# A new list of steps, other first transfers, and a 128-row product in place of a 6-row one, in a fused attention and feed-forward kernel

## The chip, the cores and the metric

One core of a Trainium2 chip runs the whole kernel. The metric is the device time of one execution in microseconds. Several runs are timed and their median is given; one further execution is profiled, and its trace is what is read here. The core has a matrix engine (TensorE, PE in the views; its weight loads, PEld, run beside the products), VectorE (DVE), ScalarE (ACT), GpSimd (POOL) and SyncE (SP, which issues the transfers).

## The reference

```python
# q, k, v: (8, 8, 576, 64) f32
scores = q @ k.T / sqrt(64)                       # per batch and head
rel = pos[:, None] - pos[None, :]
mask = (rel >= 0) & (rel < 32)                    # heads 0 to 3
mask = (rel >= 0) & (rel < 128) & (rel % 4 == 0)  # heads 4 to 7
attn = softmax(where(mask, scores, -1e9))
x = (attn @ v).transpose(0, 2, 1, 3).reshape(4608, 512)
h = x @ w_in                                      # (512, 2048), f64 given
g = h * tanh(softplus(h))                         # Mish
out = g @ w_out                                   # (2048, 512), f64 given
```

## The kernel before

The 4608 tokens are cut into 16 units of 288 (half a batch each). A unit is loaded, its scores, softmax and values are computed in four pairs of heads, the result is transposed to become the feed-forward's input, and two layers follow. In the feed-forward every number is carried as a high and a low f16 part, so that a product becomes three f16 products; the attention does the same from unit 3 on, and in f32 for units 0 to 2. From unit 4 on, two units at a time go through the first layer in a form with seven products for eight.

All engines' work is given in one list, the string `ORDER`. Each word is a step, and its instructions are issued in the list's order on each engine's own queue; a word that stands several times continues the step to its next `yield`. A number behind `=` says which of several buffers or PSUM banks (`banks`, four) the step takes. The engines wait for each other by semaphores, so a list changes when things can run, not what runs. The steps that matter here:

- `kw4`, `kw8`, `kw12`: so many products of zeros on TensorE (`keep_warm`, L1167), which nobody reads.
- `ld0`, `ld1`: q and k of a unit (L480 to L491); `lv`: its v (L511, L513). `wl0.0.1`: one block of weights, 2 x 512 KB, into one of four raw buffers (`w_load`, L372).
- `wm`, `wa` (ScalarE, L389 and L396), `ww` (VectorE, L442, L444), `ws` (TensorE L410, column sums, then VectorE), `wp` (ScalarE L455, VectorE L458): they turn a block of f64 weights into two f16 parts. `ws` needs both blocks of its group, and a raw buffer is free when `wp` is done.
- `sp`, `sc` (TensorE L680 and L683: mask and scores; VectorE L713: their maxima), `tp` (for units 0 and 1 the scores again, transposed, less the maxima, L816, then Exp), `va` (values), `tx` (transpose of the result).
- `pr`: a unit's scales. `largest` (L349) transposes the partitions' maxima (L352), reduces them (L355), puts them on the diagonal of a tile `dg` (L357) and multiplies that by ones (L360), so that every partition has them. It has 2 columns for units 0 and 1 and 6 for units 3 to 15; unit 2 goes another way.
- `ff` (first layer, L1111, units 0 to 3), `fo` (second layer, L1138), `gt` (L1126 and L1128), `ex` (Exp, units 2 and up), `za` to `zg` (first layer from unit 4 on, L1023; they and `ff` use Mish).

`wl` waits on SyncE for its raw buffer, and whatever stands behind it in SyncE's queue waits too.

Of the kernel before, what the change touches and what calls it, by code (L numbers as in the profile page):

```python
# [47 lines left out]
ld1 tp0.3=2 wp0.0.0 va0.0 kw4=1 wa0.3.1 kw8=1 ws0.3=1 tp0.3=0 va0.0=0 va0.1=2 va0.3=2 tx0.0=0 ws0.3 xa0.1=2 va0.3
wp0.3.0 va0.2=1 kw4=3 wl0.2.0=0 kw4=3 va0.2 tx0.0 sp1.1=3 tx0.0 va0.3=0 wp0.3.1 wp0.3.0 va0.2=1 sp1.0=2 sc1.1 tx0.1=1
sp1.2=3 sc1.0 tp1.0=2 tx0.0 wp0.3.1 wl0.2.1=1 wm0.2.0=0 sc1.2 tx0.1 ww0.2.0 ww0.2.0 wm0.2.1=0 tx0.1 tx0.1 ww0.2.1  # L50
wl0.1.1=2 wa0.2.0 ww0.2.1 tp1.0=1 wa0.2.1 wm0.1.1=0 wl0.1.0=3 tp1.2=0 lv2 sp1.3=3 wm0.1.0=0 sc1.3 ff0.6=1 xa1.0=3
ws0.2=2 ws0.2 ww0.1.0 ff0.7=3 ff0.7 pr1=0 ww0.1.1 ws0.1=2 ff0.6 tp1.2=0 ws0.1 pr1=0 pr1 ff0.0=2 wp0.2.0 wp0.2.1 pr1=0
wp0.2.0 ff0.0 pr1 fs0 ff0.6=0 ff0.7 va1.2=0 ff0.0=1 va1.0=1 wl1.2.0=0 va1.0 va1.2 wp0.2.1 tp1.3=3 tp1.3=1 ff0.1=2
ww0.1.1 wp0.1.1 va1.0=1 wl1.2.1=1 va1.2=3 ww0.1.0 wm1.2.0 wp0.1.1 tp1.1=3 ww1.2.0 tp1.1=0 wp0.1.0 wp0.1.0 ld2 va1.3=1
ff0.1 va1.3 va1.1=0 fs1 wm1.2.1 ff0.4=3 va1.3=2 ff0.4 va1.1 wl1.3.1=2 ff0.1 gt0.3=4 ww1.2.1 ff0.4=2 va1.1=0 ws1.2=1
tx1.0=0 ww1.2.1 tx1.0 ws1.2 tx1.1=2 ff0.5=3 ww1.2.0 gt0.3 ff0.5 tx1.1 tx1.1 gt0.0=3 tx1.0 wl1.3.0=3 pr2 ff0.2=1 ff0.5
tx1.1 ff0.2 ff0.3=3 xa3.0=4 ff0.3 wp1.2.0 wp1.2.0 tx1.0 wp1.2.1 wp1.2.1 sp2.3=2 wm1.3.0 ww1.3.0 gt0.0 sp2.1=0 ff0.2=0
ff0.3 wl1.0.0=0 sc2.3=0 sc2.1=1 wm1.3.1 gt0.2=0 ff1.2=1 ff1.6=3 ff1.6 ex2.3 ff1.2 ww1.3.1 ws1.3=2 wl1.1.1=1 ww1.3.0
ex2.1 ff1.7=0 ff1.7 gt0.2 ff1.2=1 ff1.6=2 ws1.3 gt0.1=2 wp1.3.0 tp2.3=2 ww1.3.1 sp2.2=1 ff1.7 wp1.3.0 ff1.3=3 gt0.1
sc2.2=3 ff1.3 tp2.3=1 wf1.1=0 xa2.1=1 pr2=0 pr2 wm1.0.0 ww1.0.0 wf1.1 fo0.2.0=2 wm1.1.1 ww1.1.1 fo0.2.1 sp2.0=0 ff1.3  # L60
ex2.2 fo0.2.2 sc2.0=2 wl1.0.1=3 wm1.0.1 wp1.3.1 ww1.0.1 tp2.1=3 tp2.1=0 fo0.3.0 va2.3=1 ex2.0 wp1.3.1 ww1.0.1 fo0.3.1
tp2.2=3 gt1.1=1 gt1.1 tp2.2=1 va2.1=0 ws1.0=3 va2.1 va2.3 va2.1=1 fo0.3.2 gt1.3=5 fo0.3.3 fo0.3.3=1 ws1.0 wp1.0.1
wf1.1=1 ww1.0.0 va2.2=0 va2.2 fo0.2.3 ld3 ff1.0=3 ff1.0 gt1.3 wl1.1.0=2 wm1.1.0 va2.3=0 ff1.1=1 va2.2=3 ff1.0=2 fs2
ww1.1.0 wp1.0.0 ws1.1=0 tx2.1=3 ff1.1 fo0.2.3=0 ww1.1.1 ww1.1.0 tx2.1 xa2.0=2 ws1.1 ff1.1 gt1.0=6 ff1.5=2 tx2.1 wf1.1
tx2.1 ff1.4=1 ff1.4 wp1.0.0 fo0.0.0=0 tp2.0=3 wp1.1.1 wp1.1.0 tp2.0=1 wp1.1.1 wp1.1.0 wf1.1 ff1.5 va2.0=3 ff1.4=0
ff1.5 gt1.2=7 gt1.0 lv3 wp1.0.1 fo0.0.1 fo0.0.2 wf0.0=2 gt1.2 va2.0 fo0.0.3 va2.0=3 tx2.0=2 ol pr3 pr3 fo0.2.3
fo1.2.0=1 fo1.2.1 wf1.0=0 pr3 pr3=3 wf0.0 fo0.0.3=0 mr fo0.3.3 wf1.0 fo0.0.3 fo1.2.2 pr3 pr3=3 wf0.0=1 wf0.0 pr3
fo1.2.3 pr3 fo0.1.0 xw3.0=1 wf0.1=2 pr3 pr3 wf0.0 fo1.2.3=1 fo1.2.3 pr3 pr3 ld4 fo0.1.1 fo0.1.2 fo0.1.3 pr3 tx2.0
sp3.1=3 fo1.3.0 fo1.3.1 wf1.0=1 pr3 lv4 fo0.1.3=0 sp3.0=0 tx2.0 sc3.1=2 ex3.1 tp3.1=0 pr4 sp3.3=2 sc3.3=0 fo1.3.2
fo1.3.3 sp3.2=2 fo1.0.0=3 fo1.0.1 pr4 fo1.1.0 tp3.1 ex3.3 sc3.0=1 tp3.3=1 pr4 fs3 fo1.3.3=1 ex3.0 ff2.0=0 ff2.0 wf1.0  # L70
sc3.2=3 pr4=2 pr4 tp3.1=0 xa3.1=3 ff2.1=1 wf1.0 ff2.1 tp3.0=0 tp3.0 va3.1=2 fo1.0.2 ex3.2 ff2.0=0 ff2.1 pr4=0 va3.1
wf0.1 tp3.3 pr4 va3.1 fo0.1.3 tp3.0=1 gt2.0=4 pr4 gt2.0 pr4 pr4 fo1.0.3 ff2.4=1 ff2.4 tp3.3=0 ff2.4=1 pr4 pr4 va3.0=0
tp3.2=1 fo1.3.3 pr4 ff2.5=2 ff2.5 fo1.0.3=0 ff2.5 ld5 fo1.1.1 tp3.2 tp3.2=1 sp4.0=1 fo1.1.2 va3.0 fo1.1.3 wf0.1=0
ff2.6=2 pr4 lv5 sc4.0=1 wf0.1 wf0.1 ff2.2=1 fo1.1.3=1 wf2.1=2 va3.0 xw3.1=0 va3.2=3 gt2.2=3 ex4.0 pr5 pr5 tp4.0=0
va3.2 zx3.0=0 va3.3=0 va3.3 wf2.1 va3.2 ff2.6 ff2.2 pr5 gt2.2 wf2.1=1 ff2.3=3 va3.3 zx3.0 zx3.1=1 pr5=0 wf2.1 ff2.2=2
pr5 ff2.3 ff2.3 gt2.1=2 tp4.0 fo2.2.0=0 zx3.0 pr5=3 sp4.3=1 zx3.1 zx3.1 pr5 pr5 fo2.3.0 xw4.0=2 ff2.6=0 ff2.7=3
sp4.1=2 pr5 sc4.3=2 ff2.7 sc4.1=0 gt2.1 ex4.3 fo2.0.0=1 ff2.7 ff3.2=2 ff3.2 pr5 pr5 pr5 tp4.0=1 fo2.1.0 wf2.1 ff3.2=2
ld6 pr5 sp4.2=3 sc4.2=3 sp5.0=2 xw5.0=3 fo1.1.3 fs4 fo2.2.1 va4.0=3 sc5.0=1 fo2.3.1 fo2.2.2 ff3.3=2 ex4.1 ex4.2
fo1.0.3 ex5.0 pr5 lv6 tp4.1=1 tp4.1 tp4.1=0 tp5.0=0 wf2.0=1 gt2.3=0 gt2.3 pr6 va4.0 ff3.3 ff3.3 tp5.0 fo2.1.1 fo2.1.2
fo2.1.3 va4.0 tp5.0=1 fo2.1.3=0 sp5.1=3 fo2.1.3 pr6 wf2.0 sp5.3=2 wf2.0=0 sc5.3=0 ex5.3 wf2.0 fo2.0.1 wf2.0 fo2.0.2  # L80
fo2.0.3 va4.1=2 va4.1 fo2.2.3 fo2.0.3=1 fo2.0.3 tp4.2=1 sp5.2=1 sc5.1=1 gt3.1=1 ff3.4=3 ex5.1 va4.1 gt3.1 tp5.1=0
tp5.1 ff3.4 ff3.4=1 tp5.1=0 fo2.2.3=0 ff3.5=2 va5.0=3 fo2.2.3 va5.0 tp4.2 sc5.2=1 ex5.2 ff3.5 tp4.2=1 zl2.1=0 wf3.0=2
# [1146 lines left out]
```

## Time and profile before

| | before |
|---|---|
| device time, median of 3 runs | 871.92 us |
| its runs | 871.92, 870.03, 872.19 us |
| the profiled execution's own time | 870.22 us |
| its span in the profile | 868.4 us |
| TensorE busy | 858.3 us (99%) |
| ScalarE, VectorE busy | 676.0 us (78%), 665.4 us (77%) |
| mean granted TensorE clock | 0.998 |

The span is from the first to the last instruction. TensorE's busy time is modelled from pipelined products, so that 99% does not tell how dense they are; idle time before an instruction and what ended it do. The granted clock is a share of 2.4 GHz; 0.50 is 1.2 GHz.

### The profile page before, as it was taken

How to read it: one execution, taken by the hardware profiler on the slowest of the kernel's cores; microseconds unless marked ns; L12 is line 12 of the kernel's file. 1: busy time of each engine (PE TensorE's matmuls, PEld its weight loads, DVE VectorE, ACT ScalarE, POOL GpSimd, SP SyncE). 2: the span in 40 equal slices, each digit the busy share in tenths (PEclk: the TensorE clock that was granted, in tenths of full speed). 3: DMA queues.
4: the chain of work that ended last, by engine and by line, in shares of the span. 5: the costliest groups of instructions: out<-in, count | busy, mean ns of one | idle time of the engine just before them, and what ended most of it. 6: DMA issues, size and time to landing. Idle time of an engine off the chain costs nothing.

```text
span 868.4 us, 21528 instructions
## 1 busy us (share of the span) xinstructions
PE 858.3 (99%) x8976; PEld 691.0 (80%) x8979; DVE 665.4 (77%) x1034; ACT 676.0 (78%) x978; POOL 18.5 (2%) x93
## 2 busy tenths in 40 slices
...
GB/s 257 291 192 213 131 69 158 132 176 151 142 181 192 216 196 155 216 129 174 232 144 193 167 176 173 198 166 200 189 125 181 120 188 123 132 110 155 105 8 48
DMA packets 211009, 141.20 MB, mean 163 GB/s; under 512 B 151392, under 2 KB 195936, under 8 KB 210912
## 3 DMA queue, kind: packets, MB, share of 16 engines
...
## 4 chain that ended last, share of the span: by engine, by line
PE 70%; DVE 5%; ACT 1%; issue 1%; DMA 0%; SPq 0%; DVEq 0%; ACTq 0%
PE b L1138 35%; PE b L1023 29%; PE b L857 3%; PE b L683 3%; DVE g L1128 1%; DVE p L787 1%; DVE sb L707 0%; DVE nm L713 0%; DMA out_T<-y 0%; DVE hm L969 0%; PE b L1111 0%; DVE sb L715 0%; ACT L1114 0%; ACT hm L1114 0%; DVE g L1008 0%
## 5 line engine op out<-in xcount | busy, mean ns | idle before, releaser
L1138 PE MATMUL b<-g,w 128*128 128x288 f16 x3072 | 392.8, 286 | 0.6 <-DVE g L1128 0.5
L1138 PEld LDWEIGHTS <-w 128*128 128x128 f16 x3072 | 296.1, 98 | 75.1 <-issue 1.0
L1023 PEld LDWEIGHTS <-w 128*128 128x128 f16 x2016 | 195.5, 98 | 49.6 <-issue 0.3
L1023 PE MATMUL b<-xf,w 128*128 128x288 f16 x1440 | 211.3, 286 | 0.0
L1128 DVE SCALAR_TENSOR_TENSOR g<-hm,sg,g 128x1152 f16<-128x1152 f32 x64 | 90.3, 1413 | 29.1 <-ACT g L1126 29.0
L1111 PE MATMUL b<-xf,w 128*128 128x288 f16 x768 | 99.5, 286 | 0.1
L1111 PEld LDWEIGHTS <-w 128*128 128x128 f16 x768 | 74.2, 98 | 19.5 <-issue 0.2
L1126 ACT ACTIVATE g<-hm,sg 128x1152 f16<-128x1152 f32 x64 | 80.1, 1253 | 1.0
L1152 ACT ACTIVATE y<-b,fo 128x288 f32<-128x288 f32 x60 | 42.7, 736 | 40.5 <-PE b L1138 39.7
L1033 ACT ACTIVATE hm<-hm,fs 128x576 f32<-128x576 f32 x72 | 54.1, 768 | 13.3 <-DVE hm L1084 8.6
L1023 PE MATMUL b<-w,w 128*128 128x288 f16 x288 | 63.4, 286 | 0.0
L740 ACT ACTIVATE sb<-sb,ln_p 96x768 f32<-96x768 f32 (+3 forms) x52 | 46.4, 897 | 12.7 <-DVE sb L715 12.5
L715 DVE TENSOR_TENSOR sb<-sb,nm 96x768 f32<-96x768 f32 (+4 forms) x64 | 49.2, 769 | 2.2
L713 DVE TENSOR_REDUCE nm<-sb 96x6 f32<-96x768 f32 (+4 forms) x64 | 48.8, 763 | 1.8
L787 DVE TENSOR_TENSOR p<-sb,p 96x768 f16<-96x768 f32 (+3 forms) x52 | 46.7, 903 | 4.1 <-ACT p L785 4.1
L1084 DVE TENSOR_TENSOR hm<-b,hm 128x576 f32<-128x576 f32 x24 | 18.1, 753 | 38.8 <-PE b L1023 33.8
...
L857 PEld LDWEIGHTS <-pT 128*128 128x128 f16 (+3 forms) x1092 | 38.6, 98 | 2.8 <-issue 0.6
L1023 PE MATMUL b<-xg,w 128*128 128x288 f16 x288 | 39.2, 286 | 0.0
L1006 ACT CAST w<-w 72x1024 f16<-72x1024 f32 (+3 forms) x31 | 26.0, 837 | 14.3 <-DMA xf<-w 3.3
L683 PEld LDWEIGHTS <-q 64*72 64x72 f16 (+1 forms) x1092 | 27.8, 116 | 9.3 <-issue 8.3
L1008 DVE TENSOR_TENSOR w<-w,w 72x1024 f16<-72x1024 f32 (+3 forms) x31 | 29.7, 957 | 6.6 <-ACT w L1006 6.6
...
## 6 DMA issues: line engine op xcount, KB each, us to landing
...
```

The costliest lines, as they stand in the source:

```text
L683: nc.tensor.matmul(o, q, k, start=start, stop=stop, skip_group_check=True)
L713: nc.vector.tensor_reduce(nm[:nq, :, j:j + n], x, axis=AX.X, op=ALU.max, negate=True)
L715: nc.vector.tensor_tensor(blocked(sb, c0, n, w), x, nm[:nq, :, j:j + n].unsqueeze(3).broadcast_to([nq, 2, n, w]), op=ALU.add)
L740: nc.scalar.activation(x, x, AF.Exp, bias=ln_p[:nq])
L787: nc.vector.tensor_tensor(lo, src, hi, op=ALU.subtract)
L857: nc.tensor.matmul(avv[:, h, j], pp[:nk, c:c + P], vv[vi][:nk, j, hh, :], start=(i == 0), stop=(i == 2))
L1023: nc.tensor.matmul(o[:, h, :HT], t[:, c, wi, h * P:(h + 1) * P], form_of(p, x, c, xi), skip_group_check=True, start=start and n == 0, stop ...
L1033: nc.scalar.activation(o, src, AF.Mish, scale=U[2 * p]["fs"][:, j:j + 1])
L1111: nc.tensor.matmul(ph[:, h, :HT], w1[j][c // WIDE][:, c % WIDE, wi, k * P:(k + 1) * P], x_of(d, xi, c), start=(n == 0), stop=(n == len(seq ...
L1126: nc.scalar.activation(g[:, 0], m, AF.Identity, scale=sg)
L1128: nc.vector.scalar_tensor_tensor(g[:, 1], m, sg, g[:, 0], ALU.mult, ALU.subtract)
L1138: nc.tensor.matmul(po[:, :HT], w2[:, e, j, wi, k * P:(k + 1) * P], d["g"][j][:, gi, k, :], start=(j == 0 and n == 0), stop=(j == NCH - 1 a ...
```

## The change

Three things are changed.

1. `ORDER` is written anew in its first third (to `zt2.1.2`, some 760 of 2309 steps); behind it only buffer numbers differ. The first weight block `wl0.0.1` is issued ahead of unit 0's q and k. Unit 1's `ld1` stands behind `wl0.2.0`, and its `lv1` behind `wl0.2.1`, `wl0.1.0` and `wl0.1.1` as well; both stood ahead of all four. The first feed-forward step `ff0.6` stands ahead of `tp1.2` and `sp1.3` and stood behind them.
2. The products of zeros are 152 and were 164. Before the first scores there are 76 (68 before), between the two first score steps 8 (none), before `tp0.1` none (28).
3. In `largest` the product with ones takes all 128 rows of a tile that is zero but for its first 2 or 6 rows. Three such tiles are set to zero once, on GpSimd, and used in turn.

```diff
 ORDER = """
-kw4=3 kw4=0 kw4=1 kw4=2 kw8=3 kw4=0 ld0 wl0.0.1=0 kw4=1 wm0.0.1=0 ww0.0.1 ww0.0.1 kw4=2 kw4=3 kw4=1 kw4=3 kw4=2
-xa1.1=0 kw8=0 kw4=1 kw4=3 sp0.1=2 sp0.0=0 kw4=1 sc0.1 kw4=3 kw4=1 wl0.0.0=1 wm0.0.0=0 ww0.0.0 kw4=3 ww0.0.0 kw4=1
-kw8=3 tp0.1=1 ld0 sp0.2=3 wa0.0.1 kw4=2 wl0.3.0=2 kw4=2 wa0.0.0 lv0 wm0.3.0=0 sc0.0 ws0.0=0 kw4=2 wl0.3.1=3 sc0.2
...
+kw4=3 kw4=0 kw4=3 kw12=1 wl0.0.1=0 kw4=2 ld0 kw4=0 wm0.0.1=0 kw4=0 kw4=1 kw4=3 ww0.0.1 ww0.0.1 wa0.0.1 kw4=2 kw4=1
+kw4=0 kw4=3 kw4=2 kw4=3 wl0.0.0=2 kw4=1 kw4=0 sp0.0=2 kw4=3 kw4=1 sp0.1=0 sc0.1 sc0.0 wm0.0.0=0 ww0.0.0 ww0.0.0
+wa0.0.0 tp0.1=3 kw4=0 kw4=1 kw4=2 kw4=0 ld0 sp0.3=1 ws0.0=2 ws0.0 kw4=0 tp0.1=0 wl0.3.0=1 wm0.3.0=0 kw4=0 sp0.2=0 lv0
...
+    dgs = [const.tile([P, 8], BF16, name=f"dg{i}") for i in range(3)]
+    for t in dgs:
+        nc.gpsimd.memset(t, 0.0)
+
...
         nc.vector.tensor_reduce(top[:n], t, axis=AX.X, op=ALU.max)
-        on_diagonal = pool.tile([8, 8], BF16, name="dg", bufs=3)
+        on_diagonal = dgs[0]
+        dgs.append(dgs.pop(0))
         nc.vector.tensor_scalar(on_diagonal[:n, :n], ident[:n, :n], top[:n], None, ALU.mult)
         yield
         o = single(u)[:, :n]
-        nc.tensor.matmul(o, ones_b[:n].broadcast_to([n, P]), on_diagonal[:n, :n], start=True, stop=True)
+        nc.tensor.matmul(o, ones_b.broadcast_to([P, P]), on_diagonal[:, :n], start=True, stop=True)
         yield
         return o
```

## Rows read from the trace of the kernel before

**Rows 1.** Page, part 1: busy us, share of the span, instructions.

```profile
PE 858.3 (99%) x8976; PEld 691.0 (80%) x8979; DVE 665.4 (77%) x1034; ACT 676.0 (78%) x978; POOL 18.5 (2%) x93
```

**Rows 2.** Windows: length, busy time PE, PEld, DVE, ACT, POOL; clock, DMA, GB/s.

```profile
0.00:10.00 10.00, 8.95 (x111) 8.24 (x112) 0.18 (x3) 2.55 (x6) 2.90 (x18) 1.00 0.78 246
10.00:20.00 10.00, 7.03 (x84) 5.61 (x83) 6.79 (x10) 6.77 (x9) 0.00 (x0) 0.83 0.94 267
...
45.00:252.00 207.00, 205.28 (x2154) 165.79 (x2154) 195.05 (x328) 182.50 (x276) 11.00 (x28) 1.00 0.56 153
252.00:869.00 617.00, 612.31 (x6282) 490.49 (x6280) 441.84 (x654) 464.78 (x664) 3.96 (x48) 1.00 0.64 157
```

**Rows 3.** TensorE's waits, whole span: total us, times, longest.

```profile
PE b L816 <- DVE nm L713: 2.8, 1, 2.8
...
PE b L360 <- ACT hm L1114: 0.9, 1, 0.9
```

**Rows 4.** Timeline of TensorE: start us, us, instruction, count, idle before it.

```profile
1.05 5.91 PE L1167 MATMUL b<-zeros 128*128 128x128 f16 x68 [1.05 <-DVE zeros L1162]
...
9.18 1.74 PE L1167 MATMUL b<-zeros 128*128 128x128 f16 x28
...
13.67 0.68 PE L816 MATMUL b<-ident,nm 96*128 96x96 f32 x6 [2.76 <-DVE nm L713]
...
15.92 1.24 PE L683 MATMUL b<-knd,qn 64*72 64x72 f32 x16
...
24.70 0.74 PE L683 MATMUL b<-knd,qn 64*72 64x72 f32 x16
...
44.82 1.64 PE L1111 MATMUL b<-xf,w 128*128 128x288 f16 x12
```

**Rows 5.** One window of TensorE: length, busy time, granted clock, DMA, GB/s.

```profile
16.00:17.00 1.00, 1.00 (x16) 0.50 0.92 206
```

**Rows 6.** Timeline of ScalarE, first weight passes.

```profile
9.80 1.14 ACT L389 ACTIVATE w<-raw 128x1024 f32<-128x1024 f32 x1 [6.09 <-DMA raw<-in_w_in]
12.30 1.13 ACT L389 ACTIVATE w<-raw 128x1024 f32<-128x1024 f32 x1 [1.36 <-DMA raw<-in_w_in]
```

**Rows 7.** Timeline of VectorE: its first weight pass, its first split.

```profile
10.97 0.69 DVE L442 TENSOR_SCALAR w<-w 128x1024 int32<-128x1024 int32 x1 [9.98 <-ACT w L389]
...
22.66 1.28 DVE L458 SCALAR_TENSOR_TENSOR w<-raw,ws,w 128x1024 f16<-128x1024 f32 x1
```

**Rows 8.** Timeline of SyncE's queue: when transfers are issued.

```profile
0.73 0.39 SPq L480 DMA_DIRECT2D qn<-in_qT  x1
...
1.90 2.03 SPq L372 DMA_DIRECT2D raw<-in_w_in  x4
...
26.17 0.55 SPq L482 DMA_DIRECT2D qn<-in_qT  x1
```

**Rows 9.** Weight loads by form (rows*columns): busy us, mean ns; idle before.

```profile
L683 PEld LDWEIGHTS <-q 64*72 64x72 f16 x624 | 14.3, 112 | 4.3 <-issue 3.8 <-DVE g L1008 0.2 <-DVE hm L1084 0.2
...
L857 PEld LDWEIGHTS <-pT 72*128 72x128 f16 x288 | 10.2, 97 | 0.6
...
L360 PEld LDWEIGHTS <-ones 6*128 6x128 bf16 x13 | 1.2, 90 | 3.1 <-issue 3.1
```

**Rows 10.** Timeline of weight loads around one spreading product.

```profile
342.99 0.47 PEld L1138 LDWEIGHTS <-w 128*128 128x128 f16 x4
343.69 0.09 PEld L360 LDWEIGHTS <-ones 6*128 6x128 bf16 x1 [0.24 <-issue]
343.80 0.79 PEld L857 LDWEIGHTS <-pT 128*128 128x128 f16 x24
```

**Rows 11.** L360's loads from 200 to 300 and from 300 to 700 us.

```profile
L360 PEld LDWEIGHTS <-ones x2: 90/90/90, 261.3 to 293.5; 6*128 6x128 bf16 x2
...
L360 PEld LDWEIGHTS <-ones x8: 90/90/91, 343.7 to 679.6; 6*128 6x128 bf16 x8
```

**Rows 12.** ScalarE's groups from 45 to 300 us: one kind of table load.

```profile
L1114 ACT ACT_TABLE_LOAD x11 | 14.1, 1283 | 1.1 <-DVE hm L969 1.0
```

More of the change, by code (lines that the diff above doesn't have):

```diff
@@ L48 @@
[L48 to L82, printed above, removed]
@@ new lines @@
+kw4=0 kw4=3 kw4=2 kw4=3 wl0.0.0=2 kw4=1 kw4=0 sp0.0=2 kw4=3 kw4=1 sp0.1=0 sc0.1 sc0.0 wm0.0.0=0 ww0.0.0 ww0.0.0
+wa0.0.0 tp0.1=3 kw4=0 kw4=1 kw4=2 kw4=0 ld0 sp0.3=1 ws0.0=2 ws0.0 kw4=0 tp0.1=0 wl0.3.0=1 wm0.3.0=0 kw4=0 sp0.2=0 lv0
+va0.1=3 wp0.0.1 tp0.0=2 sc0.2 tp0.2=0 wp0.0.1 sc0.3 pr0=1 pr0=1 tp0.0=0 wl0.3.1=3 ww0.3.0 kw8=2 ww0.3.0 kw4=2 tp0.2=1
+kw4=0 pr0 wm0.3.1=0 ww0.3.1 ww0.3.1 wa0.3.0 kw4=2 kw4=1 wp0.0.0 pr0=0 pr0 xa1.0=0 wa0.3.1 wp0.0.0 kw4=2 va0.0=1 va0.1
+va0.0 tp0.3=2 tp0.3=0 wl0.2.0=0 kw12=0 va0.0=0 ws0.3=0 ld1 ws0.3 wm0.2.0=0 va0.3=2 va0.3 kw4=1 xa0.1=1 wp0.3.0 va0.1=1
@@ new lines @@
+va0.3=2 va0.2=0 va0.2 tx0.0=1 sp1.1=3 wp0.3.0 xa0.0=4 tx0.0 va0.2=3 wl0.2.1=2 tx0.0 wp0.3.1 tx0.0 sp1.0=2 tx0.1=0
+tx0.1 wp0.3.1 sc1.1 sc1.0 ww0.2.0 ww0.2.0 sp1.2=1 wm0.2.1=0 ww0.2.1 ww0.2.1 wl0.1.0=1 tx0.1 tx0.1 wa0.2.0 tp1.0=3
+tp1.0=0 wa0.2.1 ff0.6=2 wm0.1.0=0 ff0.6 ws0.2=0 wl0.1.1=3 sc1.2 tp1.2=3 ws0.2 lv1 wm0.1.1=0 ww0.1.1 ww0.1.0 sp1.3=1
+wp0.2.1 wp0.2.0 pr1=1 sc1.3 ff0.7=0 ws0.1=1 wp0.2.0 ff0.7 wl1.3.0=0 ws0.1 ff0.0=1 tp1.2=1 fs0 pr1=3 wp0.2.1 ff0.0
+ww0.1.1 ff0.6=0 ff0.7 ff0.0=1 wp0.1.1 tp1.3=2 va1.0=0 pr1 pr1=3 ff0.1=1 ff0.1 ww0.1.0 pr1 wp0.1.1 tp1.3=0 va1.0
@@ new lines @@
+va1.0=3 wp0.1.0 wp0.1.0 va1.2=3 gt0.3=7 va1.2 wl1.3.1=2 va1.3=2 va1.2=1 tp1.1=0 xa2.0=2 gt0.3 xa1.1=3 ff0.2=3 wm1.3.0
+ww1.3.0 wm1.3.1 ff0.2 ww1.3.1 tp1.1=1 va1.3 ff0.1 gt0.0=0 va1.3=0 ww1.3.0 tx1.1=0 ff0.2=2 ff0.4=2 va1.1=1 tx1.1 ff0.4
+wl1.2.1=3 wm1.2.1 ff0.4=0 wl1.2.0=1 va1.1 ff0.5=3 ww1.3.1 wm1.2.0 gt0.0 ww1.2.1 tx1.1 va1.1=2 tx1.1 ww1.2.0 ff0.5
+ff0.5 ff0.3=2 gt0.2=1 ld2 tx1.0=1 tx1.0 ff0.3 ww1.2.1 fs1 tx1.0 tx1.0 ws1.3=0 ww1.2.0 gt0.2 lv2 ff0.3 gt0.1=2 sp2.3=3
+sc2.3=3 ex2.3 ws1.2=1 ws1.2 ws1.3 wp1.2.0 wp1.2.1 ff1.6=2 ff1.6 sp2.1=1 sc2.1=2 ff1.3=3 ex2.1 xa3.0=4 ff1.7=0 gt0.1
@@ new lines @@
+ff1.6=2 ff1.7 wp1.3.1 ff1.2=1 ff1.7 ff1.2 wp1.2.0 tp2.1=2 ff1.3 ff1.2=1 tp2.1=1 pr2 wp1.2.1 wf1.1=0 wl1.0.0=1 wp1.3.1
+fo0.2.0=0 tp2.3=1 ff1.3 gt1.1=3 wm1.0.0 wl1.0.1=3 wf1.1 pr2=2 pr2 wp1.3.0 wm1.0.1 va2.1=3 va2.1 gt1.1 fs2 wl1.1.0=2
+gt1.3=4 sp2.2=2 sc2.2=0 wp1.3.0 va2.1=1 ww1.0.0 wm1.1.0 wf0.0=1 ww1.0.1 ex2.2 wl1.1.1=0 xa2.1=1 fo0.2.1 fo0.2.2
+fo0.2.3 ww1.0.0 tp2.3=0 fo0.3.0 sp2.0=3 fo0.3.1 fo0.3.2 fo0.2.3=0 ws1.0=2 wm1.1.1 tp2.2=1 gt1.3 tp2.2=1 sc2.0=0
+fo0.3.3 ff1.0=1 lv3 wf0.0 ww1.1.0 fo0.3.3=1 ww1.1.1 ws1.0 ww1.1.0 va2.3=0 wf1.1=2 fo0.3.3 wp1.0.0 ff1.1=2 ff1.1 wf1.1
@@ new lines @@
+wf1.1 va2.3 ex2.0 va2.3=0 ww1.1.1 fo0.2.3 ff1.0 ff1.0=0 ws1.1=3 ws1.1 ff1.1 va2.2=0 ld3 wp1.0.0 gt1.0=5 gt1.0 tp2.0=1
+tp2.0=1 ff1.4=2 ff1.4 wp1.1.1 va2.0=3 va2.2 va2.2=2 wp1.1.1 ff1.4=2 ff1.5=1 wp1.1.0 ff1.5 va2.0 ww1.0.1 va2.0=3
+wf0.0=0 wp1.1.0 ff1.5 gt1.2=6 tx2.1=2 fo0.0.0=0 fo0.0.1 tx2.0=1 wp1.0.1 fo1.2.0=3 wp1.0.1 ol fo0.0.2 tx2.0 pr3 fo0.0.3
+pr3 wf0.0 pr3 tx2.0 fo1.3.0 fo1.2.1 wf0.1=1 gt1.2 xw3.1=1 pr3=1 fo1.3.1 fo0.0.3=0 wf0.1 pr3 pr3=1 fo0.1.0 fo0.1.1
+wf0.0 fo0.1.2 fo0.1.3 tx2.1 wf1.0=2 pr3 pr3 tx2.1 pr3 fo0.0.3 wf1.0 pr3 pr3 pr3 mr ld4 pr3 pr3 fo1.2.2 fo1.2.3 wf1.0=0
@@ new lines @@
+wf1.0 fo1.2.3=1 tx2.1 fo1.0.0=1 pr4 lv4 fo1.2.3 fo0.1.3=0 sp3.1=2 fo0.1.3 pr4 sc3.1=1 fo1.3.2 sp3.3=2 sp3.0=0 ex3.1
+tp3.1=0 sc3.3=2 fo1.1.0 tp3.1 tp3.1=0 pr4 fo1.0.1 sp3.2=2 fo1.1.1 wf0.1=2 fo1.3.3 sc3.0=0 wf1.0 xw3.0=0 ex3.3
+fo1.3.3=1 fo1.3.3 tp3.3=1 pr4=0 pr4 fo1.1.2 sc3.2=3 ex3.0 xa3.1=0 fo1.0.2 tp3.0=0 va3.1=3 ex3.2 pr4=0 pr4 ff2.1=2
+fo1.1.3 va3.1 tp3.0 tp3.0=1 ff2.0=0 pr4 fo1.0.3 ff2.0 pr4 tp3.3 va3.1 pr4 ff2.5=3 pr4 tp3.3=0 pr4 fo1.0.3=0 ld5 pr4
+tp3.2=0 wf0.1 ff2.0=0 ff2.1 fo1.1.3=1 va3.0=1 va3.0 tp3.2 ff2.1 gt2.0=0 tp3.2=1 pr4 ff2.4=0 ff2.4 va3.0 ff2.4=1
@@ new lines @@
+zx3.0=0 ff2.5 va3.3=2 gt2.0 sp4.0=1 ff2.5 ff2.2=3 va3.2=0 pr5 wf2.1=0 gt2.2=2 pr5 va3.2 wf2.1 sc4.0=1 lv5 ff2.2 zx3.0
+ex4.0 va3.2 va3.3 va3.3 gt2.2 ff2.6=1 ff2.6 sp4.3=0 sc4.3=0 pr5 ff2.2=1 ff2.3=2 ff2.3 pr5=0 wf0.1 pr5 ff2.7=3 zx3.1=1
+zx3.1 pr5=0 ff2.3 pr5 gt2.1=1 pr5 sp4.1=2 ff2.6=2 ff2.7 gt2.1 ff2.7 xw4.0=2 zx3.0 fo2.0.0=0 fo2.1.0 sc4.1=2 wf2.1=1
+sp4.2=3 wf2.1 fs3 fo1.1.3 zx3.1 tp4.0=0 tp4.0 gt2.3=3 fo1.0.3 wf2.1 tp4.0=0 fo2.1.1 pr5 ff3.3=1 fs4 ff3.3 fo2.1.2 pr5
+gt2.3 fo2.1.3 pr5 pr5 ld6 wf2.0=0 pr5 fo2.1.3=1 ff3.2=2 ff3.2 ff3.2=2 ff3.3 fo2.1.3 pr5 lv6 fo2.0.1 gt3.1=4 ex4.1
```

88 lines of the change are left out of this document (45 added, 43 removed).

## The prediction

> **What bounds the kernel now.** I read the page's shares first, then the stage windows, TensorE's waits, the start on each engine, and last the weight loads by form. TensorE is busy for 858.3 of 868.4 us [rows 1]. What is not seen there is in the windows: from 252 us to the end the loss is 617.00 - 612.31 = 4.7 us, 0.6 of it beyond the span's end and most of the rest the last output's tail; from 45 to 252 us it is 1.7 us, with VectorE (195 of 207) and ScalarE (182.5 of 207) almost as full; in the first 20 us it is 4.0 us [rows 2]. So after 45 us a microsecond of TensorE work removed is a microsecond gained, fully behind 252 us and in part before it, where VectorE may not follow. The waits say the same: the one large wait is 2.8 us for the first unit's maxima; a 0.9 us one stands before a spreading product (L360, waiting for a bank) [rows 3].
>
> In the start TensorE does three things that are not work: it runs 164 products of zeros, it waits 2.76 us at 13.67, and after that wait it runs at the lower clock: the granted clock is 0.50 (1.2 GHz) from 16 to 17 us, and the same 16 score products take 1.24 us there and 0.74 us at 24.70 [rows 4, 5]. The first 68 zero products take about 5.8 us, the 28 later ones 1.74 us, thus 0.06 us each once the engine is at speed [rows 4]. The wait's cause is the first weight block: ScalarE sat idle 6.09 us for its transfer until 9.80, VectorE could start at 10.97, and the maxima stood behind two passes over that block [rows 6, 7]. TensorE's first real products of the feed-forward start at 44.82 [rows 4].
>
> **The change, part by part.** *First transfers.* SyncE issued unit 0's q at 0.73, its k right behind, and the first weight block from 1.90 on [rows 8]; now the block goes first. Its size is 2 x 512 KB, q and k are 2 x 288 KB, and all of it has landed by 9.80 [rows 6]. In proportion to bytes from 0.73 on, the block now lands at 0.73 + 0.64 x 9.07 = 6.5 us; I take 7.0 (bounds 6.5 and 9.8). Then q and k are the last of the same bytes and land at about 9.7, in place of some time before 6.9, when their products ran. The second half of the block has the same bytes ahead of it and still comes at 12.30 [rows 6].
>
> TensorE: 76 zero products now stand before the first scores; the first 68 are out at about 6.75 (1.05 + 5.91 less the last one's tail [rows 4]), and 8 x 0.06 more make 7.2 us. From there it is idle, but for mask products, until 9.7: some 2.3 us. The two score steps took 6.9 to 9.18 = 2.3 us [rows 4]; less the mask already done, plus 8 zero products, they end at about 12.1, and VectorE, whose two passes over the first block are over by 10.5 this time, needs half a microsecond of maxima before the next step. That step starts at 12.8 to 13.2 in place of 13.67. So the wait is moved, not removed: 2.3 us before the scores and some 0.8 behind them. VectorE starts 2.8 us sooner, but the second half at 12.30 holds the column sums of the first block, so of the 2.8 only about 1 reaches the later steps. The 12 zero products fewer are 0.7 us at speed; where they stood TensorE has other things to wait for, so I count them inside this term. Start: **-1.0 us** (bounds: -4.2, if the 2.76 us, the 0.7 us and 0.7 us of low clock all go; +1.5, if new gaps cost a second stretch of low clock). The list now lets the first feed-forward product begin before two steps of unit 1 that used to stand ahead of it, so its start will move by more than the gain, to about 41.
>
> SyncE's queue: unit 1's q and k now stand behind a weight load that waits for the first raw buffer; unit 1's v stands behind three more. The first buffer was free when its split's second half, begun at 22.66 [rows 7], was over; a microsecond sooner makes 22.9, so q and k go out behind that load at 24 to 25, and they went out from 26.17 on [rows 8]. I cost this at nothing; the cover is unit 0's own work until unit 1's scores, and without it each microsecond late is one on TensorE.
>
> *Spreading the maxima.* Of the weight loads by form, those over 6 rows have 3.1 us of idle time before the 13 of them and those over 64 rows 4.3 us in one form, while 72-row ones have 0.6 us before 288 [rows 9]. One episode: four loads start 0.12 us apart, the next would be due at 343.48; the 6-row one comes at 343.69 and the next normal one at 343.80, 0.32 us late [rows 10]. With 128 rows in use the idle 0.24 us should go and a tenth of a microsecond for load and product stay. With the two 2-row ones of the start there are 15, and ten lie behind 252 us, where TensorE never waits [rows 11]: 10 x 0.24 = 2.4 us. Of the five before, two lie in the start, and I count half of the other three: 0.4 us. Together **-2.8 us** (bounds 0, if rows are not the cause, and 15 x 0.24 = -3.6). The three memsets of 128x8 on GpSimd fall into its first microseconds, before 26 us, and cost nothing; were they ahead of the mask, they would delay only a mask product that waits for q anyhow. VectorE writes the same few elements.
>
> The Trainium skill speaks against this part ("TensorE: Matmul & The Clock Gate", section "LDWEIGHTS (loading the stationary operand)"): a load's time goes with its columns and not with its rows, so that a 6-row load costs what a 128-row one does. By that rule alone the term is 0 and the sum below would be 2.8 us higher. The Trainium skill elsewhere ("TensorEngine Tiling (Array Packing)", Key Properties) has a change of tiling mode drain the array, which would leave the term as it stands. I follow the rows: the 6-row load itself takes 90 ns, no more than others, but the gap ahead of it is only there for 6 and 64 rows.
>
> *The list from 45 to 252 us.* It has another order of the same steps. Counting in the lists, ScalarE alternates between Exp and Mish 52 times before and 48 after, all four fewer in this stretch; each costs a table load of 1.283 us [rows 12], so 5.1 us of ScalarE go where it is 88% busy. TensorE waits for 1.7 us there [rows 2], 0.9 of it at a bank [rows 3]. **-0.7 us** (bounds -1.7, all waits gone, and +4, since VectorE has only 12 us to spare and any step put late on it is a new wait). Behind that stretch only buffer numbers differ, two of them exchanged throughout: 0.
>
> *Sum.* -1.0 - 2.8 - 0.7 = -4.5 us. The profiled execution took 870.22 us, so 865.7. It lies 1.7 us under the median of the runs shown, 871.92, and 0.2 over the fastest; the new median should lie above its profile in part too, by 0.8: **866.5 us**.
>
> **The rivals.** (a) Rows are not what the gap before L360 comes from (it may be a wait for VectorE's write). For it: the write comes just before. Against: 64-row loads that wait for nothing have the same gap [rows 9]. Then 866.5 + 2.8 = 869.3. It is also what the load rule of the Trainium skill's page "TensorE: Matmul & The Clock Gate" would make of it.
>
> (b) The start gains its whole bound: 866.5 - 3.2 = 863.3. For it: the old wait was a late transfer that the new list places first. Against: q and k are late now.
>
> (c) The new order makes waits between 45 and 252 us, say +3.5 against -0.7: 866.5 + 4.2 = 870.7, no measurable change. For it: VectorE at 94%. Against: four table loads fewer.
>
> (d) The other side: the clock. After the idle stretch at 7.2 to 9.7 and the short one behind the scores TensorE works in bursts, and stays at 1.2 GHz. Before, one gap of 2.76 us cost a mean clock of 0.83 over 10 us [rows 2], 1.7 us of pulses, at 1.24 against 0.74 us for a step. If the low level held from 11 to 33 us, 11 us of pulses would be lost; some of it hides in waits; +9: 875.5. It decides once the low level lasts over 14 us (half of that is 7.1 us, the forecast gain and the 0.3% together). Against: zero products fill most later gaps. The Trainium skill ("TensorE: Matmul & The Clock Gate", "What's actually happening") has the lower level as the state after idleness; the 0.50 of [rows 5] agrees.
>
> **How the numbers follow.** Forecast 0.58, (a) 0.12, (b) 0.10, (c) 0.10, (d) 0.10. A measurement of this kernel can tell about 0.3% (2.6 us) from no change: faster is under 869.3, slower over 874.5. Faster: 0.53 of the forecast, (b) 0.10, 0.07 of (a), 0.02 of (c): 0.72. Slower: 0.08 of (d), 0.01 of (c): 0.09. The same: 0.19. The range 861.5 to 871.5 leaves out (d), a part of (c), and the far end of (b): under 0.2.
>
> **What would show it.** Right: the first weight pass on ScalarE near 7 us, the first scores near 9.7, the transposed scores at about 13, the first feed-forward product near 41; no idle time before L360's loads, and the steps behind 252 us earlier by a growing amount, 0.24 us at each of ten places. Wrong: a gap still there before 128-row L360 loads; the granted clock at 0.50 beyond 20 us; TensorE's waits between 45 and 252 us over 3 us; unit 1's scores waiting for a transfer.

## The result, and the profile after

| | before | changed |
|---|---|---|
| median, 5 runs each | 871.83 us | 862.84 us |
| its runs | 870.03 to 872.19 us | 861.89 to 863.21 us |
| ratio, 95% interval | | 0.990 (0.9886 to 0.9915) |
| span of the profiled execution | 868.4 us | 861.0 us |

The change gains 9.0 us, 1.0%; the forecast was 866.5, a gain of 5.4 us, and the range held the time. In the code after, lines have moved: L352 has become L356, L360 L365, L389 L394, L442 L447, L683 L688, L713 L718, L816 L821, L857 L862, L1111 L1116, L1114 L1119, L1138 L1143, L1167 L1172.

The page, part 1, and three windows of the changed kernel, with columns as in [rows 2]:

```profile
PE 852.3 (99%) x8963; PEld 689.0 (80%) x8967; DVE 665.4 (77%) x1034; ACT 671.7 (78%) x974; POOL 19.7 (2%) x96
```

```profile
0.00:10.00 10.00, 8.24 (x108) 7.58 (x110) 2.10 (x5) 4.04 (x7) 2.98 (x22) 1.00 0.80 293
10.00:20.00 10.00, 8.66 (x127) 7.34 (x126) 6.65 (x13) 6.68 (x10) 0.00 (x0) 1.00 0.88 241
...
45.00:252.00 207.00, 206.61 (x2186) 167.93 (x2184) 199.53 (x332) 180.25 (x277) 12.68 (x29) 1.00 0.58 158
```

Against [rows 2]: the granted clock from 10 to 20 us is 1.00 (it was 0.83); from 45 to 252 us TensorE lacks 0.4 us (1.7 before), VectorE has 4.5 us more work done in the same stretch, and ScalarE 2.2 us less. Over the whole span ScalarE has four instructions fewer (974, 978 before) and 4.3 us less work; the four are table loads, 5.1 us. Two of them are missing from the group of [rows 12], which now reads:

```profile
L1119 ACT ACT_TABLE_LOAD x9 | 11.5, 1283 | 2.2 <-DVE rec L879 0.8 <-DVE g L1133 0.8 <-DVE hm L974 0.4
```

The start, in the timelines of ScalarE, of VectorE and of TensorE:

```profile
6.29 1.13 ACT L394 ACTIVATE w<-raw 128x1024 f32<-128x1024 f32 x1 [2.60 <-DMA raw<-in_w_in]
...
10.46 1.12 ACT L394 ACTIVATE w<-raw 128x1024 f32<-128x1024 f32 x1
```

```profile
7.45 0.69 DVE L447 TENSOR_SCALAR w<-w 128x1024 int32<-128x1024 int32 x1 [6.46 <-ACT w L394]
```

```profile
1.04 5.81 PE L1172 MATMUL b<-zeros 128*128 128x128 f16 x76 [1.04 <-DVE zeros L1167]
...
7.87 0.85 PE L688 MATMUL b<-knp,qn 64*96 64x128 f32 x12 [0.72 <-DMA knp<-in_kT]
...
11.23 0.68 PE L821 MATMUL b<-ident,nm 96*128 96x96 f32 x6 [0.88 <-DVE nm L718]
...
39.37 3.12 PE L1116 MATMUL b<-xf,w 128*128 128x288 f16 x24
```

The first block is there 3.5 us sooner [rows 6], and q and k come at 7.87, not at 9.7: in the first 10 us the transfers moved 293 GB/s, 246 before. The one wait of 2.76 us [rows 4] has become two of 0.72 and 0.88. TensorE is not busier for it: from 20 to 30 us it is busy for 8.69 us, 9.90 before, with new waits of 0.80 and 0.43 us. What it does in the start is at the full clock and has 12 products of zeros fewer in it.

The weight loads around one spreading product, and the eight behind 300 us:

```profile
336.89 0.71 PEld L1143 LDWEIGHTS <-w 128*128 128x128 f16 x6
337.62 0.10 PEld L365 LDWEIGHTS <-ones 128*128 128x128 bf16 x1
337.75 0.64 PEld L862 LDWEIGHTS <-pT 128*128 128x128 f16 x19
```

```profile
L365 PEld LDWEIGHTS <-ones x8: 97/98/98, 337.6 to 672.2; 128*128 128x128 bf16 x8
```

The gap of [rows 10] is gone: the load stands 0.12 us behind its neighbour and the next as much behind it. Against [rows 11] the first of the eight is 6.1 us earlier (343.7 to 337.6) and the last 7.4 us (679.6 to 672.2): seven spreadings lie between, so each gives 1.3 / 7 = 0.19 us, and 6.1 us were gained before 338 us.

### The profile page after: what moved, and what is told of

Read it like the earlier page. It is cut to its first block, busy times and chain, and to the rows that moved or that the text cites. A ratio compares the mean times of both kernels' runs of the same rounds, so it can differ in the third digit from the quotient of the medians.

```text
span 861.0 us, 21502 instructions
## 1 busy us (share of the span) xinstructions
PE 852.3 (99%) x8963; PEld 689.0 (80%) x8967; DVE 665.4 (77%) x1034; ACT 671.7 (78%) x974; POOL 19.7 (2%) x96
## 4 chain that ended last, share of the span: by engine, by line
PE 95%; ACT 1%; SPq 1%; DMA 1%; issue 0%; DVE 0%; ACTq 0%
PE b L1143 44%; PE b L1028 28%; PE b L1116 11%; PE b L688 4%; PE b L862 4%; DMA raw<-in_w_in 1%; PE b L856 1%; PE b L821 1%; SPq L518 1%; PE b L418 0%; SPq L377 0%; ACT hm L1038 0%; PE b L900 0%; SPq L516 0%; PE b L918 0%
## 5 line engine op out<-in xcount | busy, mean ns | idle before, releaser
L1143 PE MATMUL b<-g,w 128*128 128x288 f16 x3072 | 390.5, 286 | 0.0
L1143 PEld LDWEIGHTS <-w 128*128 128x128 f16 x3072 | 296.9, 98 | 74.9
L1116 PE MATMUL b<-xf,w 128*128 128x288 f16 x768 | 99.7, 286 | 0.0
L1116 PEld LDWEIGHTS <-w 128*128 128x128 f16 x768 | 73.8, 98 | 19.1 <-issue 0.2
L718 DVE TENSOR_REDUCE nm<-sb 96x6 f32<-96x768 f32 (+4 forms) x64 | 48.8, 763 | 1.8
L862 PEld LDWEIGHTS <-pT 128*128 128x128 f16 (+3 forms) x1092 | 38.7, 98 | 2.3
L688 PEld LDWEIGHTS <-q 64*72 64x72 f16 (+1 forms) x1092 | 27.8, 116 | 8.5 <-issue 7.6
```

What stands on the lines that cost most here:

```text
L688: nc.tensor.matmul(o, q, k, start=start, stop=stop, skip_group_check=True)
L718: nc.vector.tensor_reduce(nm[:nq, :, j:j + n], x, axis=AX.X, op=ALU.max, negate=True)
L862: nc.tensor.matmul(avv[:, h, j], pp[:nk, c:c + P], vv[vi][:nk, j, hh, :], start=(i == 0), stop=(i == 2))
L1116: nc.tensor.matmul(ph[:, h, :HT], w1[j][c // WIDE][:, c % WIDE, wi, k * P:(k + 1) * P], x_of(d, xi, c), start=(n == 0), stop=(n == len(seq ...
L1143: nc.tensor.matmul(po[:, :HT], w2[:, e, j, wi, k * P:(k + 1) * P], d["g"][j][:, gi, k, :], start=(j == 0 and n == 0), stop=(j == NCH - 1 a ...
```

## The experiments

The theory is that three gains add up: the start (chiefly the transfers' order), 0.19 us at each of 15 spreadings, and fewer waits in the middle, where ScalarE loads fewer tables. The rivals are that one part makes all of it, or that the zeros do. In the diffs below only the words or the main line that change are shown.

Each run also lists its mean granted clock, and the times follow it. At 0.999 or 1.000 the run had next to no stretch listed at the low clock; 0.996 is an estimated 7 us of it (0.004 x 870 us are 3.5 us of pulses, and at 0.50 half of them are lost):

| kernel | median | runs at 0.999 to 1.000: mean | runs below: mean |
|---|---|---|---|
| before (58 runs beside the experiments) | 871.2 | 10: 869.5 | 48: 871.5 |
| changed | 862.84 | 5: 862.6 | none |
| old list, rows alone | 869.44 | 2: 868.5 | 10: 869.7 |
| old list, transfers alone | 869.36 | 7: 867.9 | 5: 871.8 |
| old list, transfers and rows | 867.78 | 7: 866.9 | 5: 869.9 |
| new list, 6-row product | 865.16 | 6: 865.2 | none |
| new list, q and k first | 867.00 | none | 6: 866.7 |
| new list, no late zeros | 862.43 | 2: 861.6 | 2: 864.0 |
| new list, 12 zeros less | 865.70 | 3: 863.4 | 3: 867.8 |
| new list, no zeros | 865.60 | 2: 864.3 | 2: 866.7 |
| new list, four table loads back | 865.95 | 3: 865.9 | 1: 866.8 |
| new list, no late zeros, three steps moved | 863.47 | 2: 862.8 | 4: 863.9 |

The changed kernel was timed in one session and the others in others. Between these the mean of the kernel before at the full clock lay at 869.0 to 870.0 us, so a difference of a microsecond or less between two rows is not shown.

**Rows alone, in the old list.** The edit is the last part of the diff in the change's section, with `ORDER` as it was.

> The old list with only the spreading product over 128 rows. Main theory: the gap ahead of each 6-row load comes from the change of rows in use; it goes at all 15 places, 0.19 us each, and as TensorE is dense behind 45 us almost all of it is gained: -2.4 to -2.9 us against the kernel before, no idle time before the 15 loads. Rival (only the list matters; the gap moves to the next product or is eaten by later waits): 0 to -0.8 us.

869.44 us, ratio 0.9982 (0.9972 to 0.9992): 0.7 to 2.4 us faster. The idle time before the loads is gone, but for the one wait for a bank:

```profile
L365 PEld LDWEIGHTS <-ones x15: 97/98/98, 24.8 to 677.7; 128*128 128x128 bf16 x15
...
  ACT hm L1119: 0.9, 1
```

The last load comes 1.9 us before that of [rows 11]. Of these, 1.3 us come between the first and the last of the eight behind 300 us: 334.6 us lie between them, as in the changed kernel, where 335.9 lay in [rows 11].

```profile
L365 PEld LDWEIGHTS <-ones x8: 98/98/98, 343.1 to 677.7; 128*128 128x128 bf16 x8
```

So the part works by itself, but its time is under what was expected (2.4 to 2.9 us): 1.6 us by the ratio, 0.9 between runs at the full clock, of which there are two here.

**The new list with the 6-row product.** The small tile is taken back too.

```diff
-        nc.tensor.matmul(o, ones_b.broadcast_to([P, P]), on_diagonal[:, :n], start=True, stop=True)
+        nc.tensor.matmul(o, ones_b[:n].broadcast_to([n, P]), on_diagonal[:n, :n], start=True, stop=True)
```

> The new list with the old 6-row product. Main theory: +2.9 us against the changed kernel, so some 6 us faster than the kernel before, gaps of 0.24 us back before 14 or 15 loads. Rival (only the list matters): within 0.8 us of the changed kernel, 8 to 9 us faster than the one before. Rival (the rows are nearly all of it): under 1 us faster than the one before.

865.16 us, ratio 0.9932 (0.9914 to 0.9949), 2.3 us behind the changed kernel; the gap is back before 12 of the 15 loads, 2.8 us in all. Neither "only the list" nor "only the rows" holds.

**64 and 96 rows in the new list.** The edit for 64; that for 96 has 96 in both places.

```diff
-        nc.tensor.matmul(o, ones_b.broadcast_to([P, P]), on_diagonal[:, :n], start=True, stop=True)
+        nc.tensor.matmul(o, ones_b[:64].broadcast_to([64, P]), on_diagonal[:64, :n], start=True, stop=True)
```

> The changed kernel with the spreading product over 64 rows in place of 128. Theory that the gap comes from a change of the rows in use between two products (full array against a part of it): 0.24 us of idle time are back before nearly all of the 15 loads, as before the 64-row score products. Rival (the gap was a wait for VectorE's write of the diagonal, or belongs to very few rows): no idle time before them.

> The changed kernel with the spreading product over 96 rows. Theory that only forms of 64 rows or fewer count as another form than 128 (the trace has 72- and 104-row products without gaps): no idle time before the 15 loads. Rival (any number of rows below 128 counts): 0.24 us before each.

One run each: 864.97 and 862.73 us. The loads with 64 rows, all and those behind 300 us:

```profile
L365 PEld LDWEIGHTS <-ones x15: 92/92/93, 24.0 to 674.4; 64*128 64x128 bf16 x15
...
  issue: 2.8, 12
...
L365 PEld LDWEIGHTS <-ones x8: 92/92/93, 338.5 to 674.4; 64*128 64x128 bf16 x8
```

and with 96 rows, where no idle time is listed:

```profile
L365 PEld LDWEIGHTS <-ones x15: 97/98/126, 23.2 to 672.1; 96*128 96x128 bf16 x15
...
L365 PEld LDWEIGHTS <-ones x8: 97/98/98, 337.5 to 672.1; 96*128 96x128 bf16 x8
```

Between the first and the last of the eight lie 335.9 us with 64 rows, as with 6, and 334.6 with 96, as with 128. The operands' tiles and the writer are the same in both, so the gap is not a wait for VectorE: it comes with 64 rows or fewer (2, 6 and 64 were run) between products of the whole array, 0.23 us at 12 of 15 places, and not with 96. The Trainium skill has the engine drain at a change of tiling mode ("TensorEngine Tiling (Array Packing)", Key Properties); such a gap is what it would make, and that the mode changes at these products is not shown. Its other rule, that a load's time goes with columns ("TensorE: Matmul & The Clock Gate", "LDWEIGHTS (loading the stationary operand)"), nearly holds here: 90 ns for 6 rows, 92 for 64, 98 for 128. The gap stands ahead of the load and is not in it.

**The transfers' order alone, in the old list.**

```diff
-kw4=0 ld0 wl0.0.1=0 kw4=1
+kw4=0 wl0.0.1=0 ld0 kw4=1
```

> The old list with only the first weight block's transfer issued ahead of unit 0's q and k. Theory that the start's gain is the swap: the block lands near 6.3 us, the wait of 2.76 us before the transposed scores shrinks to about 1 us, no stretch of low clock, and 1 to 2 us are gained at the end. Rival (the swap only pays with the order of VectorE's steps made for it): the early steps move, the first feed-forward product stays near 44.8 us, 0 to -0.5 us.

869.36 us, ratio 0.9979 (0.9962 to 0.9996). TensorE's timeline:

```profile
8.01 0.85 PE L683 MATMUL b<-knp,qn 64*96 64x128 f32 x12 [0.57 <-DMA knp<-in_kT]
...
11.57 0.66 PE L816 MATMUL b<-ident,nm 96*128 96x96 f32 x6
...
41.61 1.64 PE L1111 MATMUL b<-xf,w 128*128 128x288 f16 x12
```

The transposed scores come at 11.57 without any wait, and the first feed-forward product, in the same order of steps, at 41.61 and not at 44.82 [rows 4]. The swap pays without a list made for it: 1.6 us between runs at the full clock. Five of the 12 runs had a stretch of low clock all the same (none was expected), and with it the gain was lost.

**q and k first, in the new list.**

```diff
-kw12=1 wl0.0.1=0 kw4=2 ld0 kw4=0
+kw12=1 ld0 wl0.0.1=0 kw4=2 kw4=0
```

> The new list with q and k issued first, as before. Theory that the swap makes the start's gain: the block lands near 9.8 us, the first feed-forward product moves from 39.4 to 41 us or later, +1 to +2 us against the changed kernel. Rival: the first product stays within 0.5 us of 39.4, and so does the end.

867.00 us, ratio 0.9951 (0.9934 to 0.9967), 4.2 us behind the changed kernel, twice what was expected. TensorE's timeline, and its window from 10 to 20 us:

```profile
13.33 0.68 PE L821 MATMUL b<-ident,nm 96*128 96x96 f32 x6 [3.77 <-DVE nm L718]
...
41.33 1.89 PE L1116 MATMUL b<-xf,w 128*128 128x288 f16 x14
```

```profile
10.00:20.00 10.00, 6.62 (x71) 0.83 0.90 253
```

The new list has 8 zeros between the first scores where the old one had 28 behind them, and the wait is 3.77 us; the clock falls as it did before the change, and all six runs have a mean clock under 0.999. The one at 0.998 took 864.78 us, 1.9 more than the changed kernel, as was expected; the five at 0.995 or 0.996 took 866.5 to 867.5, so the rest of the 4.2 us goes with the low clock.

**The zeros.** Without the 76 behind the first scores, and without all 152 (the `kw` words struck out):

> The changed kernel without the 76 products of zeros that stand behind the first scores. Theory that they hold the clock up: the granted clock falls to 0.50 for some microseconds between 10 and 30 us, and the end comes 0.5 to 3 us later. Rival (they stand where TensorE waits anyhow and the real products are enough for the clock): same within 1 us, or up to 1 us earlier where they delayed real products.

> The changed kernel without any of the 152 products of zeros. [...] Rival (VectorE, ScalarE and the transfers set the start, TensorE has room there): within 1 us of the changed kernel.

862.43 us, ratio 0.990 (0.9874 to 0.9926), and 865.60, ratio 0.9925 (0.9897 to 0.9952). The first expectation met half of both theories: two runs kept the full clock and took 861.6 us, 1.0 less than the changed kernel's mean, and two lost it and took 864.0. Without any zeros TensorE's windows and its timeline (L686 is L688 there) show two prices:

```profile
5.00:10.00 5.00, 2.12 (x14) 1.00 1.03 398
...
15.00:20.00 5.00, 5.00 (x42) 1.00 0.87 205
...
25.00:30.00 5.00, 3.81 (x37) 0.65 0.97 355
30.00:35.00 5.00, 5.00 (x52) 0.67 0.93 297
```

```profile
7.88 1.49 PE L686 MATMUL b<-knp,qn 64*96 64x128 f32 x12 [3.61 <-DMA knp<-in_kT]
...
16.08 1.24 PE L686 MATMUL b<-knd,qn 64*72 64x72 f32 x16
```

The first is the start. The clock is listed as 1.00 there, but the 12 score products take 1.49 us where they take 0.85 in the changed kernel, and 16 of the other form take the 1.24 us that they took at 0.50 in [rows 4, 5]; in these 20 us the column does not show how fast the engine runs. The second is the listed low clock between 25 and 35 us. Two of the four runs list a mean clock of 1.000, which leaves the first price in: they took 863.7 and 864.9 us, 1.7 more than the changed kernel on the mean. So the first 76 zeros bring the first scores to speed, and the later ones carry the clock over 25 us.

Last, without one word of 12 zeros, which stands before column sums that need the same bank:

```diff
-kw12=0 va0.0=0 ws0.3=0
+va0.0=0 ws0.3=0
```

> The changed kernel without the 12 zero products before the column sums of w_in's fourth block (they wait 0.8 us for the same bank as the sums and then run 0.7 us ahead of them). Theory from the run without late zeros (half of its runs keep the full clock and are 1 us faster, half fall to a mean clock of 0.996 and lose 2.4 us): these 12 cost up to 0.7 us and do not guard the clock, so the runs stay at a clock of 0.999 to 1.0 and end 0.3 to 0.7 us sooner, 862.2 to 862.5. Rival (any of the late zeros guards the clock): some runs fall to 0.996 and 864 to 865. Rival (the sums wait for ScalarE anyhow): no change.

865.70 us, ratio 0.9928 (0.9906 to 0.995): slower than the changed kernel by 2.9 us. The theory fell. TensorE's windows in this kernel, and then in the changed one:

```profile
26.00:28.00 2.00, 0.72 (x12) 1.00 1.00 370
28.00:30.00 2.00, 1.06 (x6) 0.91 0.82 243
30.00:32.00 2.00, 2.00 (x19) 0.50 0.81 237
...
34.00:36.00 2.00, 2.00 (x13) 0.50 0.36 96
```

```profile
26.00:28.00 2.00, 1.20 (x23) 1.00 1.01 380
28.00:30.00 2.00, 1.49 (x14) 1.00 0.78 217
30.00:32.00 2.00, 2.00 (x33) 1.00 0.92 281
```

After the thinner stretch the clock is 0.50 (1.2 GHz) and only 19 products begin in two microseconds where 33 did. Three of six runs went this way, at 867.8 us. The late zeros are an insurance. In the new list with the large rows first, 16 of 17 runs with all the late zeros have a mean clock of 0.999 or more, and 7 of 16 without some or all of them; those that lose it take 2.4 us more in the run without late zeros and 4.4 here. What the zeros cost is not shown beyond noise: 1.0 us by the two runs without them, nothing by the last version below (862.8 at the full clock). The Trainium skill has the lower level as the state after idleness ("TensorE: Matmul & The Clock Gate", "What's actually happening"); the run without any zeros agrees (no product begins from 25 to 26 us, and the clock is 0.50 from 27), and the rows here show that a stretch with some work in it can end so too.

**Transfers and rows together, in the old list.** Both edits from above.

> The old list (164 products of zeros) with the two other parts: the first block's transfer ahead of q and k, and the 128-row product. By the profiles of the two parts alone (3.2 and 1.9 us) their sum is 5 us: 866 to 867. Theory that the new order of the middle is worth 2 to 3 us by itself (fewer waits between 45 and 290 us): it stays 3 to 4 us behind the changed kernel. Rival (the order is worth nothing beside the swap and the rows): within 1 us of the changed kernel, 863.

867.78 us, ratio 0.9971 (0.9956 to 0.9985), 4.9 us behind the changed kernel. The order of the steps, with the zeros, is worth that much beside the two other parts; 4.3 us between runs at the full clock. The weight loads' waits from 45 to 300 us, in this kernel and then in the changed one, and last TensorE's windows in this kernel:

```profile
PEld L688 <- issue: 3.3, 10, 1.2
PEld L1143 <- issue: 1.0, 2, 0.7
PEld b L688 <- issue: 1.0, 4, 0.3
PEld L862 <- issue: 0.8, 1, 0.8
```

```profile
PEld L688 <- issue: 2.4, 10, 0.2
PEld b L688 <- issue: 1.3, 5, 0.3
PEld b L356 <- issue: 0.6, 1, 0.6
```

```profile
45.00:252.00 207.00, 204.54 (x2153) 1.00 0.55 152
45.00:870.00 825.00, 813.36 (x8422) 1.00 0.60 156
```

With the smaller lines the sums are 7.7 and 5.0 us. TensorE itself is idle for 2.5 us from 45 to 252 us, and for 0.4 in the changed kernel. So 2.1 us of the difference are waits of the middle. Of the 3.5 us between the two spans (864.5 and 861.0) the other 1.3 lie ahead of 45 us: TensorE has 813.4 us of work left there, and 812.0 in the changed kernel. That much is not put down to the order, because two traces with the old start differ by it too: the first feed-forward product comes at 42.93 here and at 41.61 with the transfers alone.

**Four table loads put back.**

```diff
+"te": lambda i: nc.scalar.activation(first, ln_p, AF.Exp),
-ff2.6=2 ff2.7 ff2.7
+ff2.6=2 te0 ff2.7 ff2.7
-ff3.2=2 ff3.3
+ff3.2=2 te1 ff3.3
```

> The changed kernel with two more Exp of 128x1 on ScalarE, one after the Mish of ff2.6 and one after that of ff3.2; nobody reads them, and each makes ScalarE load Exp's table and then Mish's again: 4 loads of 1.28 us and 0.4 us of work, 5.5 us of ScalarE near 180 to 210 us. Theory that the fewer table loads made the middle's gain: +1 to +4 us, with new waits of TensorE between 180 and 260 us. Rival (ScalarE has that room): within 0.5 us.

865.95 us, ratio 0.9944 (0.9928 to 0.996): 3.1 us behind the changed kernel for 5.5 us of ScalarE. TensorE's waits have three new lines:

```profile
PE b L862 <- ACT hm L1119: 1.8, 1, 1.8
PE b L688 <- ACT hm L1119: 1.1, 1, 1.1
...
PE b L688 <- ACT y L1157: 0.7, 1, 0.7
```

They make 3.6 us, all with ScalarE as the one waited for. ScalarE has no room at these two places, though it was busy for 88% of the stretch. That the four loads of the old list cost as much at theirs is not shown: of the three waits of TensorE in that list's middle (0.9, 0.5 and 0.5 us) only the first [rows 3] is for ScalarE.

**A version that might beat both.** Without the 76 late zeros, and with `sp3.0` moved to stand before `sp3.2`, `sp6.3` before `sp6.1`, `sp14.3` before `sp15.1`.

> The changed kernel without the 76 zero products behind the first scores, and with three score steps put right before another one (sp3.0 before sp3.2, sp6.3 before sp6.1, sp14.3 before sp15.1), so that the array's rows in use change three times less. Theory: 1.1 us from the zeros as in the profile of the run without them, 3 x 0.24 us from the steps: 1.5 to 2 us faster than the changed kernel, 861. Rival (a step put later delays its maxima and what follows, or the zeros' gain was noise): within 0.5 us of the changed kernel, or slower.

863.47 us, ratio 0.9914 (0.9899 to 0.993): no better than the changed kernel. The idle time before the score products' loads did fall, from 4.3 to 4.0 us in each of two forms, but four of six runs had a mean clock under 0.999, and the two others took 863.35 and 862.30 us, where the changed kernel's runs lie between 861.89 and 863.21. None of the kernels was shown to be faster than the changed one.

## Why the prediction was right, and where its sizes were off

The time lay in the range and the direction was right, but the gain was 9.0 us for a forecast of 5.4, and the time lies only 1.3 us inside the range's lower end. Between runs at the full clock the change gains 869.5 - 862.6 = 6.9 us, and the rest, 2 us, is low clock that the kernel before has in 48 of 58 runs and the changed one in none of its five. The 0.8 us added for a median above the profile did not come: the changed kernel's profiled run is its median.

How the gain divides in the profiled runs can be estimated from TensorE's work left at 45 us, in the kernel before, in the new list with the 6-row product, and in the changed kernel (the windows reach past the spans):

```profile
45.00:870.00 825.00, 817.59 (x8434) 1.00 0.62 156
45.00:870.00 825.00, 815.10 (x8440) 1.00 0.63 156
45.00:870.00 825.00, 812.04 (x8428) 1.00 0.61 156
```

The start is 817.6 - 815.1 = 2.5 us, the spreading 815.1 - 812.0 = 3.1, and the middle's idle time, 1.7 before and 0.4 after, 1.3. With 0.5 us less idle time behind 252 us these make the 7.4 us between the two spans. The median of the kernel before lies another 1.6 us above its profiled run.

**Start, forecast -1.0.** The mechanism was right, the size was not, and this is the term that was mis-sized most: 2.5 us in the profiled runs, and about 4 with the 1.6 us of the median. The step that failed is the landing in proportion to bytes: 7.0 us and 9.7 us were taken, 6.29 and 7.87 came, and the second half, held to stay at 12.30, was worked on at 10.46. So there was no idle stretch of 2.3 us before the scores, and the transposed scores came at 11.23, not 12.8. The swap alone is 1.6 us at the full clock. The low clock I had as 0.7 us inside a bound; it is 2 us in the median.

**Spreading, forecast -2.8.** Right in kind: 1.3 / 7 = 0.19 us each where I took 0.24, and 15 of them make 2.9. Of the 0.32 us of an episode, 0.13 stay (the load at 337.62 to the next at 337.75), which leaves 0.19. Measured in the new list it is 2.3 us in the medians and 3.1 between the profiled runs, in the old one 0.7 to 2.4. Rival (a) fell with the 64- and 96-row products.

**Middle, forecast -0.7, bound -1.7.** Right in kind and short: against the kernel before, TensorE's idle time there fell by 1.3 us; against the old list with the two other parts, by 2.1, which is past the bound. The bound took the waits of [rows 2] as fixed, but the same list waits 2.5 us there once the other two parts are in. I had called VectorE the engine without room and given ScalarE's 5.1 us no price; put in at two places, such loads cost 3.1 us. Which of the new list's moves makes the gain (the four table loads, unit 1's moved transfers, the earlier first feed-forward step) is not separated by any run.

**Rivals.** (b), the start's whole bound, came nearest in time (863.3) and mostly by its own way: the start gained about 4 of its 4.2 us, the wait of 2.76 us shrank to 1.6 in two parts, and the low clock went. (c) had the sign wrong: TensorE waits 1.3 us less between 45 and 252 us. (d) did not happen in the changed kernel, but its mechanism is real: q and k first in the new list, no zeros, no late zeros, or 12 zeros less each brought a stretch of low clock in some or all runs, at some 2.4 us and more.

**The signs named ahead** held in the main: no gap before 128-row loads, steps behind 300 us earlier by a growing amount (0.19 us at each place, not 0.24), no low clock beyond 20 us, no late transfer for unit 1, TensorE's waits between 45 and 252 us at 0.4. The times of the start did not: the first scores came at 7.87 where 9.7 stood, the transposed ones at 11.23 where 13 stood, and the first feed-forward product at 39.4 where 41 stood.
